# A set order for the first attention batch: scores ahead of attn x v, first keys copied in two parts, transposes and h blocks moved around its end

## Chip, cores, metric

The kernel runs on one core of a Trainium2 chip. The metric is the device time of one execution in microseconds (us). The span in a profile (first to last instruction) is about 1.8 us shorter than the time of the same execution.

## The reference

```python
def _attn_ref(q, k, v):                      # q, k, v: (8, 12, 448, 64)
    scores = scale * np.matmul(q, k.transpose(0, 1, 3, 2))
    attn = np.maximum(scores, 0.0) ** 2 / S
    return np.matmul(attn, v)

def _moe_ref(x, w_in, w_out):                # x: (3584, 768), w_in: (768, 2048), w_out: (2048, 768)
    h = x @ w_in
    r = np.maximum(h, 0.0)
    return (r * r) @ w_out
```

The attention output, laid out as 3584 x 768, is the x of the second function. The types taken and given are float32. The kernel works in float16 with float32 sums.

## The kernel before

A batch is three units (four heads each), a unit seven score tiles, so a batch has 21 tiles, 0 to 20. For each unit TensorE transposes q and k, and VectorE copies them out of PSUM, the memory that TensorE's results go to. For each tile TensorE makes the scores, ScalarE evicts them (copies them out of PSUM, here with relu, to float16), VectorE squares them, and TensorE multiplies them with v, summed over the seven tiles of the unit. Two copies then write x. The first batch has no other work to hide behind. Later batches lie among the matmuls of h (x @ w_in) and the output. The units 0 to 5 are transposed by TensorE; from unit 6 on, a transposing DMA transfer does it.

The parts that matter here (cuts marked `# ...`):

```python
def slot(dtype):                       # score and transpose buffers, two banks each
    slot_no[0] += 1
    third = not big and slot_no[0] % 3 == 2 and slot_no[0] < 29
    return (third_p if third else s_p).tile(...)

def pe_transpose(n):
    # ... 14 transposes of q and 14 of k into PSUM
        if n == 0:
            copy(i)                    # all seven blocks in one VectorE copy
            warm(1)                    # a filler matmul
    # ...
    if n == 3:
        return lambda: (copy(0, True), copy(1))   # ScalarE for q, VectorE for k

def score(t, times=1):
    # ... four matmuls, done `times` times over, then:
    nc.scalar.activation(out=at, in_=ps[:, :, 0:S], func=AF.Relu, scale=SK)

def visit(tiles, turn=None, lag=2, most=3):
    # ... first batch:
    for t in tiles:
        score(t, 2)                    # twice, which keeps TensorE busy
    if turn is not None:
        pe_transpose(turn)
    flush()
    av_some(lag, most)                 # attn x v of tiles that are two visits old
    for t in tiles:
        square(ats[t])
    flush()

warm(10)
pe_transpose(0)
for i in range(11):
    visit([t for t in (2 * i, 2 * i + 1) if t < NB0], turn={1: 1, 4: 2}.get(i))
    # ... loads
later = pe_transpose(3)
# ... loads of v and w_out, then of unit 6 and 7
av_some(1, 9)
some(f0[0:2])                          # f0, f1: h blocks 0 and 1, six matmuls each
later()
av_some(0, 9)
# ...
some(f0[2:4])
some(f1[0:2])
visit([NB0, NB0 + 1])                  # scores 21 and 22, of unit 3
```

## Time and profile before

| | before |
|---|---|
| time, median of 3 | 372.46 us (372.42 to 372.77) |
| span of the profile, granted TensorE clock | 370.7 us, 0.996 |
| first eviction of a score tile | 8.26 us |
| end of the 21st eviction | 26.26 us |
| scores 23 and 24 (the first after h block 2) | 31.51 us |
| first scores of unit 6 | 68.75 us |

Most of the reading of this profile is in the prediction below. What it leaves out is the seam after the batch. It is the continuation of the chain of waits that ended last (columns: start in us, length in us, what; `x4` counts instructions):

```profile
26.97 0.48 PE mm L423 x2
27.46 0.31 PE avt L273 x4
27.77 0.86 PE mm L423 x4
28.64 0.50 PE slot L255 x8
29.14 2.38 PE mm L423 x12
31.51 0.50 PE slot L255 x8
```

`mm` are h steps, `avt` is attn x v, `slot ... L255` are scores. TensorE stands nowhere here, so this stretch can be shortened only by moving work of it to an earlier time at which TensorE was idle. The start of the last row, 31.51 us, is the mark by which the two kernels can be compared, as from there on their order is the same.

### The profile page before, as it was taken

How to read it: one execution, taken by the hardware profiler on the slowest of the kernel's cores; microseconds unless marked ns; L12 is line 12 of the kernel's file. 1: busy time of each engine (PE TensorE's matmuls, PEld its weight loads, DVE VectorE, ACT ScalarE, POOL GpSimd, SP SyncE). 2: the span in 40 equal slices, each digit the busy share in tenths (PEclk: the TensorE clock that was granted, in tenths of full speed). 3: DMA queues.
4: the chain of work that ended last, by engine and by line, in shares of the span. 5: the costliest groups of instructions: out<-in, count | busy, mean ns of one | idle time of the engine just before them, and what ended most of it. 6: DMA issues, size and time to landing. Idle time of an engine off the chain costs nothing.

```text
span 370.7 us, 8742 instructions
## 1 busy us (share of the span) xinstructions
PE 361.1 (97%) x3600; PEld 230.9 (62%) x3600; DVE 266.0 (72%) x470; ACT 247.7 (67%) x370; POOL 107.1 (29%) x128
## 2 busy tenths in 40 slices
PE   8999999999999999999999999999999999999994
PEld 3554444445555778875555588887555689986663
DVE  1886677996767878798575766989756686884442
ACT  2997895786667999876555588887665885532220
POOL 8545531747542355522054045050000000000001
PEclk9999999999999999999999999999999999999998
DMA  8999999999999999969799999592233300002333
GB/s 116 195 204 205 205 204 170 126 146 161 190 170 137 185 106 104 108 90 73 137 136 108 176 162 94 82 104 48 54 82 88 87 1 2 2 0 79 91 91 83
DMA packets 121158, 42.63 MB, mean 115 GB/s; under 512 B 100832, under 2 KB 117760, under 8 KB 121120
## 3 DMA queue, kind: packets, MB, share of 16 engines
q0 software_dynamic: 82912, 23.01, 63.7%
q1 hardware_dynamic: 38048, 18.98, 25.8%
q8 instruction: 28, 0.46, 0.5%
q10 hardware_dynamic: 160, 0.10, 0.1%
q14 instruction: 10, 0.08, 0.1%
HBM read 45.61 MB, written 11.01 MB: 153 GB/s over the span
## 4 chain that ended last, share of the span: by engine, by line
PE 90%; ACT 4%; DVE 3%; issue 1%; POOL 0%; POOLq 0%; ACTq 0%
PE mm L739 34%; PE mm L552 27%; PE slot L255 10%; PE mm L423 9%; PE slot L320 7%; ACT at L259 4%; DVE at L372 1%; PE slot L204 1%; PE slot L226 1%; DVE xt L286 1%; PE mm L226 0%; DVE kT L217 0%; ACT u L641 0%; DVE osb L646 0%; PE avt L273 0%
## 5 line engine op out<-in xcount | busy, mean ns | idle before, releaser
L259 ACT ACTIVATE at<-slot 128x896 f16<-128x896 f32 x168 | 145.9, 919 | 27.9 <-PE slot L255 27.8
L372 DVE TENSOR_TENSOR at<-at 128x896 f16<-128x896 f16 x168 | 99.3, 618 | 12.1 <-ACT at L259 12.0
L109 POOL DMA_DIRECT2D qs<-in_q_dram x36 | 35.3, 983 | 116.5 <-DMA qT<-qs 108.7
L739 PEld LDWEIGHTS <-s 128*128 128x128 f16 x440 | 41.5, 98 | 32.7 <-issue 3.6
L255 PE MATMUL slot<-qT,kT 64*64 64x448 f16 x756 | 57.4, 360 | 1.6 <-ACT at L259 0.9
L552 PEld LDWEIGHTS <-w 128*128 128x128 f16 x576 | 54.3, 98 | 5.1 <-issue 4.3
L552 PE MATMUL mm<-xt,w 128*128 128x224 f16 x432 | 48.9, 259 | 0.0
L739 PEld LDWEIGHTS <-g 128*128 128x128 f16 x336 | 31.7, 98 | 24.1 <-issue 4.7
L552 PEld LDWEIGHTS <-ws 128*128 128x128 f16 x432 | 40.3, 98 | 4.7 <-issue 4.7
L646 DVE SCALAR_TENSOR_TENSOR osb<-mm,u 128x384 f32<-128x384 f32 (+1 forms) x30 | 16.2, 543 | 36.2 <-ACT u L641 23.7
L739 PE MATMUL mm<-b,g 128*128 128x384 f16 x224 | 40.7, 326 | 0.0
L739 PE MATMUL mm<-b,s 128*128 128x384 f16 x216 | 39.6, 326 | 0.2 <-DVE s L608 0.2
L423 PE MATMUL mm<-xt,w 128*128 128x448 f16 x192 | 39.8, 354 | 0.0
L739 PE MATMUL mm<-t,s 128*128 128x384 f16 x224 | 39.3, 326 | 0.0
L255 PEld LDWEIGHTS <-kT 64*64 64x64 f16 x756 | 19.6, 104 | 28.9 <-issue 23.6
L109 POOL DMA_DIRECT2D ks<-in_k_dram x36 | 35.1, 977 | 8.4 <-DMA b<-in_moe_w_out_dram 5.8
L575 POOL DMA_DIRECT2D out_dram<-osb x2 | 1.1, 564 | 119.7 <-DVE osb L646 119.7
L641 ACT ACTIVATE u<-mm 128x384 f32<-128x384 f32 x28 | 13.8, 492 | 31.3 <-PE mm L739 26.8
L552 PE MATMUL mm<-x,ws 128*128 128x224 f16 x288 | 34.1, 259 | 0.0
L495 DVE CUSTOM_DVE_ANT_0 g<-mm,m 128x448 f16<-128x448 f32 x36 | 22.4, 622 | 14.9 <-PE mm L552 7.2
L320 PE MATMUL slot<-at,vt 64*64 64x448 f16 x588 | 31.9, 350 | 0.2 <-DVE at L372 0.2
L501 DVE TENSOR_TENSOR g<-g 128x896 f16<-128x896 f16 x48 | 28.8, 618 | 0.4 <-ACT g L504 0.4
(68 smaller groups left out, 378.1 us busy)
## 6 DMA issues: line engine op xcount, KB each, us to landing
out_dram<-osb SPq DMA_DIRECT2D x52, 192.0 KB, 3.0
vt<-in_v_dram POOLq DMA_DIRECT2D x24, 224.0 KB, 6.0
qs<-in_q_dram POOLq DMA_DIRECT2D x36, 112.0 KB, 4.4
ks<-in_k_dram POOLq DMA_DIRECT2D x36, 112.0 KB, 5.2
w<-in_moe_w_in_dram POOLq DMA_DIRECT2D x8, 384.0 KB, 11.7
b<-in_moe_w_out_dram POOLq DMA_DIRECT2D x4, 768.0 KB, 17.1
q<-in_q_dram POOLq DMA_DIRECT2D x6, 224.0 KB, 7.6
k<-in_k_dram POOLq DMA_DIRECT2D x6, 224.0 KB, 8.1
```

Of the source, the lines that this page charges most:

```text
L109: nc.gpsimd.dma_start(out=t[:, :, hh, :], in_=heads(src, n)[:, hh].rearrange("p (j d) -> p j d", d=D))
L255: nc.tensor.matmul(ps[c, hh, 0:S], lhsT=kT[r, j, c], rhs=qT[r, :, c], start=True, stop=True)
L259: nc.scalar.activation(out=at, in_=ps[:, :, 0:S], func=AF.Relu, scale=SK)
L320: nc.tensor.matmul(ps[64 * hh:64 * hh + 64, hp, 0:S], lhsT=vt[r, hh, j * D:(j + 1) * D], rhs=at[r, hh, :], start=(j == 0), stop=(j == J - 1))
L372: lambda: nc.vector.tensor_mul(at, at, at), 0))
L423: nc.tensor.matmul(cell[0][:, 0:S], lhsT=w1[f // 4][:, m, (f % 4) * P:(f % 4 + 1) * P], rhs=xts[b][:, m, :], start=(m == 0), stop=(m == NM ...
L495: nc.vector._custom_dve(TENSOR_ADD_SAT, out=gs(s, hi, right), in0=acc(s, y), in1=keep[s, nm], s0=3.4e38, s1=0.0)
L501: lambda: nc.vector.tensor_mul(g, g, g), b))
L552: nc.tensor.matmul(XY[s][y][:, r * Q:(r + 1) * Q], lhsT=left(k, i0 + 2 * s + r, m), rhs=right(k, m), start=(fresh and r == 0 and m == 0), ...
L641: nc.scalar.activation(out=t, in_=X[0][:, 0:HALF], func=AF.Copy, scale=CO)
L646: nc.vector.scalar_tensor_tensor(out=osb[row][:, c], in0=acc[0][:, 0:cc.stop - cc.start], scalar=CO, in1=keep[nm][:, cc], op0=ALU.mult, op ...
L739: nc.tensor.matmul(acc[0][:, 0:HALF], lhsT=left()[:, f], rhs=right[:, f], start=(fresh and f == 0), stop=(f == KH - 1), skip_group_check=n ...
```

## The change

The loop over visits of the first batch is replaced by a list of calls. Its intent: let ScalarE begin sooner, never let it wait for a score, and give TensorE work while the last squares and copies run. The diff, cut to its core:

```diff
-    def slot(dtype):
-        slot_no[0] += 1
-        third = not big and slot_no[0] % 3 == 2 and slot_no[0] < 29
+    def slot(dtype, third=False):
...
+    def turn_first(ps):
+        ts = new_qkt()
+        for i, src in enumerate(q16s.pop(0)):
+            tps = slot(FP16)[:, i, 0:J * P].rearrange("p (j c) -> p j c", j=J)
+            # 14 transposes
+            if i:
+                nc.scalar.activation(out=ts[i][:, 0], in_=tps[:, 0], func=AF.Copy)
+            nc.vector.tensor_copy(ts[i][:, i:J], tps[:, i:J])
+            warm(ps, 1)
+        qkt[0] = ts
...
-            return lambda: (copy(0, True), copy(1))
+            return lambda: copy(0, True), lambda: copy(1)
...
-    for i in range(11):
-        visit([t for t in (2 * i, 2 * i + 1) if t < NB0], turn={1: 1, 4: 2}.get(i))
+    s(0, 1)          # s(t, times=2): a score; THIRD = (0, 3, 5, 8, 10, 13, 16, 19)
+    s(1)
+    s(2)
+    s(3)
+    square0(0, 1)
+    pe_transpose(1)
+    s(4, 1)
+    s(5)
+    square0(2)
+    av0(0, 1)
+    s(6)
+    square0(3)
+    s(7)
+    av0(2)
...                  # on in this way; s(9, 1) behind pe_transpose(2)
+    s(19)
+    later = pe_transpose(3)
+    square0(17)
+    s(20)
+    av0(14, 15, 16, 17)
+    square0(18, 19, 20)
+    later[0]()
...
-    av_some(1, 9)
-    some(f0[0:2])
-    later()
-    av_some(0, 9)
+    some(f0[0:4])
+    av0(18, 19, 20)
+    x0(2, 0, act=True)
+    x0(2, 1)
+    later[1]()
+    some(f1[0:4])
...
-    some(f0[2:4])
-    some(f1[0:2])
+    some(f0[4:6])
     visit([NB0, NB0 + 1])
```

More of the change, by code (lines that the diff above doesn't have):

```diff
@@ L192, with warm @@
     wsum: dict = {}
-    slot_no = [0]
-    def slot(dtype):
-        slot_no[0] += 1
-        third = not big and slot_no[0] % 3 == 2 and slot_no[0] < 29
+    def slot(dtype, third=False):
         return (third_p if third else s_p).tile(
             [P, 2, 2048 // mybir.dt.size(dtype)], dtype, name="slot", tag="slot")
-    def warm(n):
-        ps = slot(FP32)
+    def warm(ps, n):
         for _ in range(n):
@@ L205, in warm @@
                              start=True, stop=True)
+    def turn_first(ps):
+        ts = new_qkt()
+        for i, src in enumerate(q16s.pop(0)):
+            tps = slot(FP16)[:, i, 0:J * P].rearrange("p (j c) -> p j c", j=J)
+            for j in range(J):
+                for hh in range(2):
+                    nc.tensor.transpose(
+                        tps[64 * hh:64 * hh + 64, j],
+                        src[:, hh, j * D:(j + 1) * D], ident)
+            if i:
[3 more added lines that the diff above has]
+        qkt[0] = ts
     def pe_transpose(n):
@@ L221, in pe_transpose @@
         else:
-            pss = [ps, slot(FP16) if n == 0 else ps]
+            pss = [ps, ps]
         for i, src in enumerate(srcs):
@@ L228, in pe_transpose @@
                         src[:, hh, j * D:(j + 1) * D], ident)
-            if n == 0:
-                copy(i)
-                warm(1)
         qkt[n] = ts
         if n == 3:
-            return lambda: (copy(0, True), copy(1))
-        if n > 0:
-            copy(0, n > 3)
-            copy(1)
+            return lambda: copy(0, True), lambda: copy(1)
+        copy(0, n > 3)
+        copy(1)
     xts: dict = {}
@@ L243, with score @@
     now = [0]
-    av_order: deque = deque(range(NU * J))
     avt = [None]
-    def score(t, times=1):
+    def score(t, times=1, third=False):
         n, j = divmod(t, J)
         qT, kT = qkt[n]
-        ps = slot(FP32)
+        ps = slot(FP32, third)
         for hh in list(range(2)) * times:
@@ L261, in score @@
         seen[t] = now[0]
-    def av_round(t):
-        n, j = divmod(t, J)
-        b, u = divmod(n, NU)
-        vt, at = vts[n], ats.pop(t)
-        if j == 0:
-            avt[0] = [p.tile([P, 512], FP32, name="avt", tag="av") for p in av_ps]
-        ap = avt[0]
-        for hp in range(2):
-            r = slice(64 * hp, 64 * hp + 64)
-            for hh in range(2):
-                nc.tensor.matmul(
-                    ap[hp][64 * hh:64 * hh + 64, 0:S],
-                    lhsT=vt[r, hh, j * D:(j + 1) * D], rhs=at[r, hh, :],
-                    start=(j == 0), stop=(j == J - 1))
-        if j == J - 1:
-            if u == 0:
-                xts[b] = x_p.tile([P, NM, S], FP16, name="xt", tag="xt")
-            for hp in range(2):
-                dst = xts[b][:, 2 * u + hp, :]
-                if b < 2 and u == NU - 1 and hp == 0:
-                    nc.scalar.activation(
-                        out=dst, in_=ap[hp][:, 0:S], func=AF.Copy, scale=CX)
-                else:
-                    nc.vector.tensor_scalar(
-                        out=dst, in0=ap[hp][:, 0:S],
-                        scalar1=CX, scalar2=None, op0=ALU.mult)
@@ L290, in av_some, with av0 @@
-    def av_some(lag=2, most=3):
-        done = 0
-        while av_order and done < most:
-            t = av_order[0]
-            if t not in seen or seen[t] > now[0] - lag:
-                break
-            av_order.popleft()
-            av_round(t)
-            done += 1
-            if t % J == J - 1:
-                break
+    def av0(*tiles):
+        for t in tiles:
+            n, j = divmod(t, J)
+            vt, at = vts[n], ats.pop(t)
+            if j == 0:
+                avt[0] = [p.tile([P, 512], FP32, name="avt", tag="av") for p in av_ps]
+            for hp in range(2):
+                r = slice(64 * hp, 64 * hp + 64)
+                for hh in range(2):
+                    nc.tensor.matmul(
+                        avt[0][hp][64 * hh:64 * hh + 64, 0:S],
+                        lhsT=vt[r, hh, j * D:(j + 1) * D], rhs=at[r, hh, :],
+                        start=(j == 0), stop=(j == J - 1))
@@ new lines, in x0, with square0 @@
+    def x0(n, hp, act=False):
+        if 0 not in xts:
+            xts[0] = x_p.tile([P, NM, S], FP16, name="xt", tag="xt")
+        dst, src = xts[0][:, 2 * n + hp, :], avt[0][hp][:, 0:S]
+        if act:
+            nc.scalar.activation(out=dst, in_=src, func=AF.Copy, scale=CX)
+        else:
+            nc.vector.tensor_scalar(
+                out=dst, in0=src, scalar1=CX, scalar2=None, op0=ALU.mult)
+    def square0(*tiles):
+        for t in tiles:
+            nc.vector.tensor_mul(ats[t], ats[t], ats[t])
@@ L372, in square, with visit @@
                     lambda: nc.vector.tensor_mul(at, at, at), 0))
-    def visit(tiles, turn=None, lag=2, most=3):
+    def visit(tiles):
         now[0] += 1
@@ L378, in visit @@
                 prefetch(t // J + 2)
-        if big:
-            for t in tiles[:1]:
-                score(t)
-            av_unit()
-            for t in tiles[1:]:
-                score(t)
-            at_pe[0] += 0.19 + 0.19 * len(tiles)
-            for i, t in enumerate(tiles):
-                square(ats[t], 0.6 + 0.85 * i)
-            return
-        for t in tiles:
-            score(t, 2)
-        if turn is not None:
-            pe_transpose(turn)
-        flush()
-        av_some(lag, most)
-        for t in tiles:
-            square(ats[t])
-        flush()
+        for t in tiles[:1]:
+            score(t)
+        av_unit()
+        for t in tiles[1:]:
+            score(t)
+        at_pe[0] += 0.19 + 0.19 * len(tiles)
+        for i, t in enumerate(tiles):
+            square(ats[t], 0.6 + 0.85 * i)
     gts: dict = {}
@@ L789, with s @@
     NB0 = NU * J
-    warm(10)
-    pe_transpose(0)
-    for i in range(11):
-        visit([t for t in (2 * i, 2 * i + 1) if t < NB0], turn={1: 1, 4: 2}.get(i))
-        if i == 0:
-            load16(3)
-            load_w1(0)
-            load_w1(1)
-            load_v(3)
-        if i == 2:
-            load16(4)
-            load_w1(2)
-            load_v(4)
-        if i == 5:
-            load16(5)
-            load_w1(3)
-            load_v(5)
-    later = pe_transpose(3)
+    ps = slot(FP32, True)
+    warm(ps, 10)
+    turn_first(ps)
+    def s(t, times=2):
+        score(t, times, third=t in THIRD)
+    THIRD = (0, 3, 5, 8, 10, 13, 16, 19)
+    s(0, 1)
[4 more added lines that the diff above has]
+    pe_transpose(1)
+    load16(3)
+    load_w1(0)
+    load_w1(1)
+    load_v(3)
+    s(4, 1)
[6 more added lines that the diff above has]
+    av0(2)
+    square0(4)
+    s(8)
+    av0(3)
+    square0(5, 6)
+    pe_transpose(2)
+    load16(4)
+    load_w1(2)
+    load_v(4)
+    s(9, 1)
+    square0(7)
+    s(10)
+    av0(4, 5)
+    square0(8)
+    s(11)
+    av0(6)
+    x0(0, 0)
+    x0(0, 1)
+    square0(9)
+    load16(5)
+    load_w1(3)
+    load_v(5)
+    s(12)
+    s(13)
+    square0(10, 11)
+    s(14)
+    av0(7, 8, 9)
+    square0(12)
+    s(15)
+    av0(10)
+    square0(13)
+    s(16)
+    av0(11)
+    s(17)
+    av0(12, 13)
+    square0(14)
+    x0(1, 0)
+    x0(1, 1)
+    s(18)
+    square0(15, 16)
+    s(19)
+    later = pe_transpose(3)
+    square0(17)
[3 more added lines that the diff above has]
+    later[0]()
     load_v(6)
@@ L902 @@
         events.append((2 * T_H - (3 - i) * T_G, lambda i=i: outs[0][1](i)))
-    steps = [(0.1892, None, False)] * 6 + f1[2:4] + f0[4:6] + f1[4:6]
+    steps = [(0.1892, None, False)] * 10 + f1[4:6]
     for f in range(2, NF):
```

## The prediction

> **What bounds the kernel now.** I read the page first, then the chain of waits around the first batch, then each engine's timeline there, then the DMA queue up to the first use of data that comes through it late.
>
> The change touches only the first attention batch (21 score tiles) and its seam with the first h blocks, that is, the first 30 us of 370.7. Three engines' busy time in that stretch (engines: busy us, instructions in brackets):
>
> ```profile
> core 0: us, PE busy (x) PEld busy (x) DVE busy (x) ACT busy (x) POOL busy (x), PEclk, DMA share, GB/s
> 8.20:26.30 18.10, 16.13 (x320) 9.92 (x308) 15.63 (x29) 17.39 (x21) 9.17 (x14) 1.00 1.23 197
> ```
>
> ScalarE (ACT) is nearest to its limit, 17.39 of 18.10 us, all of it the 21 relu evictions of score tiles; VectorE (DVE) has 15.63 us for 29 instructions. So no order of work inside this stretch can win more than about 0.7 us: the rest must come from its start and its end. ScalarE's timeline (start, us, what, idle before) shows where its 0.7 us goes:
>
> ```profile
> 8.26 8.27 ACT L259 ACTIVATE at<-slot 128x896 f16<-128x896 f32 x10 [6.02 <-PE slot L255]
> 16.87 3.35 ACT L259 ACTIVATE at<-slot 128x896 f16<-128x896 f32 x4 [0.34 <-PE slot L255]
> 20.48 5.78 ACT L259 ACTIVATE at<-slot 128x896 f16<-128x896 f32 x7 [0.27 <-PE slot L255]
> 26.51 0.92 ACT L215 ACTIVATE qT<-slot 128x896 f16<-128x896 f16 x1 [0.25 <-PE slot L226]
> ```
>
> Ten evictions in 8.27 us with a last one of 0.92 give a pitch of (8.27 - 0.92)/9 = 0.82 us. Twenty pitches are 16.3 us; from 8.26 the 21st would start at 24.6 and it starts at 25.34 (20.48 + 6 x 0.81), so 0.7 us are gaps, behind the transposes of unit 2 and the x copies. The chain that ended last (start, us, what) says what follows:
>
> ```profile
> 7.64 0.60 PE slot L255 x8
> 8.24 0.02 issue
> 8.26 6.66 ACT at L259 x8
> ...
> 15.97 0.62 DVE qT L217
> 16.60 0.53 DVE kT L217
> 17.13 1.07 DVE at L372 x2
> 18.20 1.06 DVE xt L286 x2
> ...
> 24.49 0.97 ACT at L259
> 25.46 0.04 issue
> 25.50 0.97 PE slot L226 x28
> 26.47 0.50 PE avt L273 x8
> ```
>
> Before 25.5 the path runs through ScalarE and VectorE. From 25.50 on TensorE (PE) sets it: the transposes of unit 3 (0.97 us) stand after all 21 scores. From there it runs almost without a wait to the end of the kernel, so what is gained before about 30 us should be gained at the end, unless something arrives by a clock of its own. One thing does: DMA is fully busy from 4 to 62 us, and unit 6's keys come through it.
>
> ```profile
> 61.48 1.23 SPq L120 DMA_TRANSPOSE kT<-ks  x1
> DMA to landing us min/median/max: 5.8/5.8/5.8
> 68.75 0.50 PE slot L255 x8
> ```
>
> The first row is the issue of the transposing transfer of these keys, the second its time to landing (so 67.3), the third the matmuls that read them.
>
> **What the Trainium skill says.** "ScalarE: Activation LUTs", section "What ACT_TABLE_LOAD costs", puts an ACTIVATE at a fixed part plus 0.833 ns per element. The trace agrees: 0.919 us for 896 columns and 0.544 for 448, a slope of 0.837 ns and 0.17 us fixed, so an estimate of 0.28 us for the new copy of 128 columns. "PSUM — Partial Sum Buffer", section "PSUM bank collisions raise a hardware error", says two engines must not read one bank at once, so ScalarE's and VectorE's parts of the first key copy should run one after the other. No copy of before shows this. "TensorE: Matmul & The Clock Gate", section "The mechanism" of Part 3, says matmuls start and end in program order. The trace agrees: at 18.78 and 23.45 us the attn x v matmuls stood waiting for an x copy, and the scores behind them stood too (0.7 us of TensorE waits on x copies in three waits). That is what putting scores ahead of attn x v addresses.
>
> **The change, part by part.**
>
> Start. Before: keys transposed by 6.94, one VectorE copy of all seven key blocks 6.96 to 7.60, scores 7.64 to 8.24 (each computed twice, eight matmuls), first eviction 8.26. After: ScalarE copies block 0 alone, 6.96 to 7.24. TensorE is free from 7.21, after the filler matmul. Score 0 is computed once, four matmuls, 0.38 us: 7.27 to 7.65. First eviction 7.67, so 0.6 us earlier. VectorE copies the other six blocks, 7.26 to about 7.8, score 1 is ready at 8.4, and the second eviction is due at 7.67 + 0.82 = 8.49: no gap.
>
> Middle. The same instructions in a fixed order with three rotating score buffers, plus three scores computed once instead of twice (3 x 4 matmuls at about 0.05 us, 0.6 us off TensorE). I walked the order by hand with 0.82 per eviction, 0.54 per VectorE instruction, 0.97 per set of 28 transposes, 0.57 per double score. Each score found its buffer free and was ready before ScalarE asked, also behind the transposes of units 1 and 2 (at about 9.4 and 13.5 us; the data of unit 2 land at 13.3). So up to 0.7 us of gaps go. The last eviction then ends at 7.67 + 16.3 + 0.92 = 24.9 instead of 26.26. VectorE is close behind: 29 x 0.54 = 15.6 us from 8.6 on, plus about 1.3 us in which it waits for transposes and evictions, so the last square is done at about 25.5 (before: 26.9).
>
> End. The 28 transposes of unit 3 come before score 20, as soon as a buffer frees at about 22.5, while ScalarE still has three evictions to do. Four steps of h block 0 run before the last attn x v, four of block 1 after it. Then: last attn x v 25.9, x copies 26.6, VectorE's key copy 27.1, scores 21 and 22 to 27.6, last two steps of block 1 to 28.0. Before, h block 1 ended at 29.14 + 6 x 0.2 = 30.3. That is 2.3 us in a walk without any slip. A walk by hand misses semaphore delays and short queues, so I take 1.5 to 2.3, middle 1.8, of which 0.6 is the start, about 0.6 gaps, about 0.6 the end. No arithmetic of any size is removed.
>
> Downstream. From 30 us the order is as before, shifted. The first scores of unit 6 start at 68.7; their keys land at 67.3 by the DMA's clock. Their issue waited for data in a queue that has been full since 4 us, so the shift won't move it. The slack is 68.7 - 67.3 = 1.4 us. A shift of 1.8 would run into it by about 0.4, and a short semaphore and weight-load delay of about 0.1 comes on top. So I expect about 1.3 us to survive: 372.46 - 1.3 = 371.15.
>
> **The rivals.**
> First, the DMA does not cap it: the keys land earlier too, or only a part is needed, and all 1.8 us arrive, 370.7. Against: the landing of each transfer follows the bytes ahead of it at about 204 GB/s; for: a few instructions that free load buffers come earlier, and landing times could vary by half a microsecond.
> Second, VectorE takes ScalarE's place as the bound in the first batch. Its 15.63 us already lies on the chain at 16 to 21 us. If the late squares hold up the attn x v and those the x copies, the gaps come back and only the start's 0.6 us plus a little of the end remains: 371.7.
> Third, the wait moves: ScalarE's share of the key copy might make score 0 wait for the whole key tile, which would leave score 0 at 7.85 and make the start worse by 0.2 less 0.2 for the single computing. For region-wise waits speaks that h steps reading x blocks 2 and 3 ran at 27.70, ahead of the copies into blocks 4 and 5 (27.81 and 28.00), which stand before them in the program. That rival gives about 371.8.
> A slower kernel would need TensorE's clock to drop after fewer double scores; with 16.13 of 18.10 us busy before and 0.6 us less after, in three places, I see no pause long enough.
>
> **Range and chances.** Point 371.15, between the cap (1.3) and what survives if the first batch yields less. The low end, 370.6, is the full shift without a cap; the high end, 371.8, is the start alone. Two per cent is 7.4 us, more than the whole of what this stretch could give: within 2% is as good as certain, 0.98, and 0.01 for each side.
>
> **What would show each step right or wrong.** First eviction at about 7.7 us, a ScalarE copy of 0.28 us at about 7.0 and VectorE's part following it: the start. ScalarE's evictions in one run to about 25 us: the middle; gaps named after score matmuls would speak for the second rival. The end of h block 1 at 28.0 to 28.8 us instead of 30.3: the end. A TensorE wait of some tenths before the scores at about 67.3 us, released by the key transfer or by nothing visible: the cap; none there and a span shorter by over 1.5 us: the first rival. The prediction is wrong if the shift at 30 us is below 0.8 us, or if a shift over 1.5 us there reaches the end undiminished.

## The result, and the profile after

| | before | after |
|---|---|---|
| time, median of 4 runs each | 372.6 us | 370.66 us (370.6 to 371.21) |
| span, clock | 370.7 us, 0.996 | 368.9 us, 0.998 |
| first eviction | 8.26 us | 7.72 us |
| end of the 21st eviction | 26.26 us | 24.90 us |
| scores 23 and 24 | 31.51 us | 29.73 us |
| first scores of unit 6 | 68.75 us | 66.97 us |
| last part of the output matmuls | 364.31 us | 362.53 us |

The ratio is 0.9951, with a 95% interval of 0.9934 to 0.9969. Ratios here are the mean time of one kernel's fast runs over that of the other's of the same rounds, so not quite the ratio of the medians quoted. The kernel is about 0.5% faster, by the profile 1.8 us. The forecast was 1.3.

Busy time in the first batch after (same columns as in the prediction), from 0.12 us before the first eviction to 0.5 us behind the end of the last (the 22nd ScalarE instruction is the copy of unit 3's queries):

```profile
7.60:25.40 17.80, 16.00 (x316) 10.05 (x312) 16.04 (x30) 17.68 (x22) 9.55 (x15) 1.00 1.23 195
```

ScalarE now has 17.68 of 17.80 us: by busy time it is full. Its timeline shows the 21 evictions as one row, where before had three rows with 0.34 and 0.27 us between them (a row ends only where the engine stands idle, so a short delay can hide in it; see "The middle" below):

```profile
6.96 0.28 ACT L214 ACTIVATE kT<-slot 128x128 f16<-128x128 f16 x1 [4.72 <-PE slot L210]
7.72 17.18 ACT L266 ACTIVATE at<-slot 128x896 f16<-128x896 f32 x21 [0.49 <-PE slot L262]
24.80 0.91 ACT L227 ACTIVATE qT<-slot 128x896 f16<-128x896 f16 x1
```

The first row is the new small copy. VectorE's part of the key copy follows it and does not overlap it:

```profile
7.27 0.56 DVE L215 COPY kT<-slot 128x768 f16<-128x768 f16 x1 [0.70 <-ACT kT L214]
```

The chain of waits around the end of the batch after:

```profile
22.46 0.97 PE slot L238 x28
23.43 0.50 PE slot L262 x8
23.94 0.76 PE avt L280 x16
24.69 0.86 PE mm L409 x4
25.55 0.69 PE avt L280 x12
26.25 1.26 PE mm L409 x6
27.50 0.03 issue
27.54 0.57 PE slot L262 x8
28.11 1.62 PE mm L409 x8
29.73 0.50 PE slot L262 x8
```

The transposes of unit 3 (first row) start at 22.46 instead of 25.50, and from there TensorE runs without a pause to scores 23 and 24 at 29.73.

The 1.78 us divide as follows. The first eviction is 0.54 us earlier (8.26 to 7.72). From its start to the end of the 21st eviction it takes 17.18 us instead of 18.00, so 0.82. The mark at 31.51 moved to 29.73, which leaves 1.78 - 0.54 - 0.82 = 0.42 us for the end. The same 1.78 us stand at the scores of unit 6 and at the output's last part: nothing is lost on the way. The cap that the prediction put at 67.3 us did not act. The issue of the transposing transfer of unit 6's keys, its time to landing, and the scores that read them:

```profile
61.88 1.23 SPq L120 DMA_TRANSPOSE kT<-ks  x1
DMA to landing us min/median/max: 4.4/4.4/4.4
66.97 0.50 PE slot L262 x8
```

The issue did not come earlier; it came 0.4 us later than before (61.48). But the transfer landed after 4.4 us instead of 5.8, at 66.3, and 0.7 us of slack remained: the keys lay ready 0.7 us before the scores that read them.

### The profile page after: what moved, and what is told of

Read it like the earlier page. It is cut to its first block, busy times and chain, and to the rows that moved or that the text cites. A ratio compares the mean times of both kernels' runs of the same rounds, so it can differ in the third digit from the quotient of the medians.

```text
span 368.9 us, 8720 instructions
## 1 busy us (share of the span) xinstructions
PE 359.6 (97%) x3588; PEld 230.3 (62%) x3588; DVE 265.4 (72%) x470; ACT 247.5 (67%) x371; POOL 107.1 (29%) x128
## 4 chain that ended last, share of the span: by engine, by line
PE 90%; ACT 3%; DVE 3%; issue 2%; DMA 1%; POOL 0%; POOLq 0%; ACTq 0%
PE mm L725 34%; PE mm L538 27%; PE slot L262 10%; PE mm L409 9%; PE slot L317 7%; ACT at L266 3%; DMA k<-in_k_dram 1%; DVE at L297 1%; PE avt L280 1%; PE slot L238 1%; PE mm L238 0%; DVE at L369 0%; DVE xt L292 0%; ACT u L627 0%; DVE osb L632 0%
## 5 line engine op out<-in xcount | busy, mean ns | idle before, releaser
L369 DVE TENSOR_TENSOR at<-at 128x896 f16<-128x896 f16 x147 | 87.1, 617 | 9.7 <-ACT at L266 9.6
L538 PEld LDWEIGHTS <-w 128*128 128x128 f16 x576 | 54.3, 98 | 5.1 <-issue 4.3
L409 PEld LDWEIGHTS <-w 128*128 128x128 f16 x192 | 17.1, 98 | 19.2 <-issue 5.1
```

The lines of the kernel that those rows point to most:

```text
L369: lambda: nc.vector.tensor_mul(at, at, at), 0))
L409: nc.tensor.matmul(cell[0][:, 0:S], lhsT=w1[f // 4][:, m, (f % 4) * P:(f % 4 + 1) * P], rhs=xts[b][:, m, :], start=(m == 0), stop=(m == NM ...
L538: nc.tensor.matmul(XY[s][y][:, r * Q:(r + 1) * Q], lhsT=left(k, i0 + 2 * s + r, m), rhs=right(k, m), start=(fresh and r == 0 and m == 0), ...
```

## The experiments

All twelve kernels gave correct results. The table gives the median of each and the marks of its profile. "Batch" is the time from the first eviction to scores 23 and 24: 23.25 us before, 22.01 after. It takes out the start, which moves by some tenths from profile to profile with the landing of the first keys. "Slower by the medians" below is measured against the changed kernel's median in again, 370.69. best2 ran on another chip than the other eleven.

| kernel | median us | before, same rounds | ratio | batch us | scores of unit 6 | keys: issue + landing = landed |
|---|---|---|---|---|---|---|
| again | 370.69 | 372.52 | 0.9957 | 22.00 | 66.8 | 62.37 + 4.4 = 66.8 |
| start_only | 372.11 | 372.52 | 0.9987 | 23.26 | 68.05 | 62.27 + 5.7 = 68.0 |
| mid_old | 371.44 | 372.52 | 0.9973 | 22.82 | 67.7 | 61.50 + 4.4 = 65.9 |
| t3_late | 371.07 | 372.52 | 0.9964 | 22.43 | 67.7 | 62.79 + 4.4 = 67.2 |
| h_old | 371.25 | 372.52 | 0.9966 | 22.51 | 67.5 | 61.55 + 4.4 = 66.0 |
| k_whole | 370.95 | 372.52 | 0.9966 | 22.00 | 67.2 | 61.49 + 4.4 = 65.9 |
| dbl0 | 370.87 | 372.52 | 0.9960 | 22.00 | 67.1 | 61.46 + 4.4 = 65.9 |
| dbl49 | 371.11 | 372.52 | 0.9967 | 22.13 | 67.26 | 61.44 + 5.8 = 67.2 |
| dma_after | 371.07 | 372.55 | 0.9964 | 22.01 | 67.1 | 62.61 + 4.4 = 67.0 |
| dma_before | 372.53 | 372.55 | 1.0006 | 23.25 | 68.6 | 63.24 + 4.4 = 67.6 |
| best | 370.79 | 372.55 | 0.9954 | 21.99 | 67.0 | 61.56 + 4.4 = 66.0 |
| best2 | 370.51 | 372.42 | 0.9956 | 21.82 | 66.43 | 57.81 + 8.1 = 65.9 |

The intervals of the ratios are about 0.0013 to 0.0022 to each side, that is 0.5 to 0.8 us. So differences of some tenths between these kernels rest on their medians together with the marks of the profiles, not on the intervals. One cause of the width is that single executions fall on a second level some 0.4 to 0.7 us higher, whatever the kernel. In the first job before had 372.19 to 372.55 seven times and 372.93 and 373.07 once each. Single executions lie higher still (372.71 in k_whole, 372.36 in best2).

One reading settles which kernels lost time to unit 6's keys: the scores of unit 6 start 37.24 to 37.26 us after scores 23 and 24 in thirteen of the fourteen profiles, and 37.42 us after them in dbl49.

### again: the changed kernel once more

No edit.

> The changed kernel once more, unchanged. Theory (the 1.8 us won by 30 us reach the end, because the keys of unit 6 happened to land within reach): 1.7 to 1.95 us faster than before, the scores of unit 6 starting at 66.9 to 67.1 us. Rival (the landing of these keys varies from run to run and caps the gain in some executions): the keys land anywhere between 66 and 67.4 us, and single executions are 0.3 to 0.6 us longer than the best.

Measured: 370.69 us, 1.83 below before by the medians. The keys landed at 66.8 us, just when the scores of unit 6 came (66.8), so the slack was used up, at no cost: they start 37.25 us after scores 23 and 24, as elsewhere. Two of five executions were longer (371.02 and 371.17; the others 370.65 to 370.69). That agrees in form with the rival, but before has the same second level, and its slack is larger. So the longer executions are no sign of the cap.

### start_only: only the start of the change

```diff
+                if i:
+                    nc.scalar.activation(out=d3[:, 0], in_=p3[:, 0], func=AF.Copy)
+                nc.vector.tensor_copy(d3[:, i:J], p3[:, i:J])
                 warm(1)
...
-            score(t, 2)
+            score(t, 2 if t else 1)
```

(in the kernel before; `d3` and `p3` are views of the key tile and of its PSUM)

> The kernel before with only the start of the change: ScalarE copies the first key block, score 0 computed once. Theory (the start's 0.54 us are worth themselves, and the gaps and the end are separate gains): first eviction at 7.7 us, 0.4 to 0.6 us faster than before. Rival (VectorE bounds the middle anyway, so an earlier start only opens wider gaps in ScalarE): first eviction at 7.7 us, but under 0.2 us faster.

Measured: 0.41 us faster than before by the medians, first eviction at 7.53. In its profile the first eviction and scores 23 and 24 are 0.73 and 0.72 us earlier than before, as its first keys came 0.19 us earlier. ScalarE's timeline has the very gaps of before:

```profile
7.53 8.27 ACT L263 ACTIVATE at<-slot 128x896 f16<-128x896 f32 x10 [0.49 <-PE slot L259]
16.14 3.35 ACT L263 ACTIVATE at<-slot 128x896 f16<-128x896 f32 x4 [0.34 <-PE slot L259]
19.75 5.77 ACT L263 ACTIVATE at<-slot 128x896 f16<-128x896 f32 x7 [0.27 <-PE slot L259]
```

So an earlier start shifts the batch as a whole (23.26 us against 23.25), and the gaps are a separate matter. The theory holds.

### mid_old: the old order in the middle

The list from score 0 to score 17 in the order of the old visits, for instance:

```diff
-    s(8)
-    av0(3)
-    square0(5, 6)
-    pe_transpose(2)
-    s(9, 1)
-    square0(7)
-    s(10)
-    av0(4, 5)
+    s(8)
+    s(9, 1)
+    pe_transpose(2)
+    av0(4, 5)
+    square0(8, 9)
+    s(10)
```

> The changed kernel with the middle of the batch in the old order of tiles, attn x v and squares (start and end as changed). Theory (the set order closes ScalarE's gaps): gaps of 0.4 to 0.8 us come back in the row of 21 evictions, last eviction at 25.3 to 25.7 instead of 24.9, 0.4 to 0.8 us slower than the changed kernel. Rival (the gaps came from scores computed twice behind transposes, which this version keeps single): no gap over 0.1 us, within 0.15 us of the changed kernel.

Measured: 0.75 us slower than the changed kernel by the medians, 0.81 in the batch. The gaps are back, at the same places and of the same size as before, although three scores are computed once:

```profile
7.63 8.21 ACT L266 ACTIVATE at<-slot 128x896 f16<-128x896 f32 x10 [0.49 <-PE slot L262]
16.17 3.35 ACT L266 ACTIVATE at<-slot 128x896 f16<-128x896 f32 x4 [0.34 <-PE slot L262]
19.79 5.84 ACT L266 ACTIVATE at<-slot 128x896 f16<-128x896 f32 x7 [0.27 <-PE slot L262]
```

What makes the second gap is seen on TensorE. An attn x v there waits for the x copy to free its accumulator, and the scores behind it in the program start only after it:

```profile
18.09 0.38 PE L280 MATMUL avt<-at,vt 64*64 64x448 f16 x2 [0.38 <-DVE xt L292]
18.62 0.76 PE L280 MATMUL avt<-at,vt 64*64 64x448 f16 x10 [0.15 <-DVE xt L292]
19.03 1.10 PE L262 MATMUL slot<-qT,kT 64*64 64x448 f16 x16
```

ScalarE's gap at 19.5 us lies just behind these rows. The first gap, at 15.8 us, has another cause: score 10 stands behind the transposes of unit 2 (from 14.27) and eight attn x v matmuls (from 15.17), and starts at 15.57. In both places it is the order that makes ScalarE wait. The theory holds; the rival falls for these two gaps (dbl49 shows what the single scores are worth).

### t3_late: the transposes of unit 3 after score 20

```diff
-    later = pe_transpose(3)
     square0(17)
     s(20)
+    later = pe_transpose(3)
     av0(14, 15, 16, 17)
```

> The changed kernel with the transposes of unit 3 after score 20, as before. Theory (TensorE sets the path from 22.5 us on, and these transposes then start when the next buffer frees, at 23.3): h block 1 ends about 0.25 us later, 0.2 to 0.4 us slower than the changed kernel. Rival (the squares of the last tiles set the end, at 25.6 us, whatever TensorE does before): within 0.1 us of the changed kernel.

Measured: 0.38 us slower by the medians, as expected, and 0.42 in the batch. TensorE's timeline shows how:

```profile
22.71 0.57 PE L262 MATMUL slot<-qT,kT 64*64 64x448 f16 x8 [0.24 <-ACT at L266]
23.52 0.58 PE L238 MATMUL slot<-ident,q 128*64 128x128 f16 x14 [0.24 <-ACT at L266]
```

Score 20 takes the buffer that frees first, takes 0.57 us on TensorE, and the transposes then wait 0.24 us for the next. In the changed kernel the transposes take the first buffer, and score 20's wait for the second one falls into the transposes' own 0.97 us.

### h_old: the h blocks as before

```diff
-    some(f0[0:4])
+    some(f0[0:2])
     av0(18, 19, 20)
...
-    some(f1[0:4])
...
-    some(f0[4:6])
+    some(f0[2:4])
+    some(f1[0:2])
     visit([NB0, NB0 + 1])
```

(the remaining steps behind the scores, as in the kernel before)

> The changed kernel with the steps of h blocks 0 and 1 around the last attn x v and the scores of unit 3 as before (two steps ahead of the last attn x v, four after, the rest behind scores 21 and 22). Theory (h steps fill TensorE while the last square, the x copies and the last key copy run; without them it stands): TensorE idle 0.4 to 0.8 us between 25 and 27.6 us, 0.4 to 0.7 us slower than the changed kernel. Rival (the same steps are done later in the same queue, where they fill other waits): under 0.15 us slower.

Measured: 0.56 us slower by the medians, 0.50 in the batch. The chain of waits leaves TensorE here, as TensorE has too few h steps to do while the last x copy and the key copy run:

```profile
25.17 0.87 PE avt L280 x12
26.05 0.02 issue
26.07 0.62 DVE xt L292
26.69 0.54 DVE kT L229
27.23 0.04 issue
27.28 0.57 PE slot L262 x8
```

Score 21 starts earlier than in the changed kernel (27.28 against 27.54), and still the mark behind the h steps is later, as four of the ten steps that the changed kernel has done by then are still to do. TensorE's idle time before score 21 is 0.42 us, within what was expected.

### k_whole, dbl0: the two parts of the start

```diff
-            if i:
-                nc.scalar.activation(out=ts[i][:, 0], in_=tps[:, 0], func=AF.Copy)
-            nc.vector.tensor_copy(ts[i][:, i:J], tps[:, i:J])
+            nc.vector.tensor_copy(ts[i][:, 0:J], tps[:, 0:J])
```

> The changed kernel with the first keys copied whole by VectorE. Theory (the start shifts everything up to the end of the batch one to one): first score at 7.64 instead of 7.29, first eviction at 8.05 instead of 7.72, 0.3 to 0.35 us slower than the changed kernel. Rival (VectorE, not ScalarE, sets the end of the batch; its first squares come later but its total has room): under 0.15 us slower.

```diff
-    s(0, 1)
+    s(0)
```

> The changed kernel with score 0 computed twice. Theory (score 0 is on the path): first eviction at 7.9 instead of 7.72, 0.15 to 0.25 us slower than the changed kernel. Rival (the 0.5 us that the second score waits for the other key blocks absorbs it): no difference over 0.05 us.

Measured: 0.26 and 0.18 us slower by the medians. The starts of the first keys' copy and of the first eviction are 6.96 and 7.72 in the changed kernel (0.76 us apart), 6.83 and 7.94 in k_whole (1.11), 6.88 and 7.83 in dbl0 (0.95). That is 0.35 and 0.19 us. The rest of the batch is unchanged in both (22.00). Both theories hold; only k_whole's 0.26 by the medians is just under its expected 0.3 to 0.35.

### dbl49: the other two scores computed twice

```diff
-    s(4, 1)
+    s(4)
...
-    s(9, 1)
+    s(9)
```

> The changed kernel with the two scores behind the transposes of units 1 and 2 computed twice, as before. Theory (ScalarE asks for these scores 0.2 to 0.3 us after they are ready even when doubled by 0.19 us, so they are not on the path): within 0.1 us of the changed kernel. Rival (this is what closed the gaps): gaps of 0.1 to 0.2 us at the fifth and the tenth eviction, 0.2 to 0.4 us slower.

Measured: 0.42 us slower by the medians, outside what the theory expected and just above the rival's range. The rival is right about the place: by the start times in the trace, the fifth eviction starts 0.89 us after the fourth and the tenth 0.91 after the ninth, where the changed kernel has 0.80 in both. So each is late by about 0.1 us, too little to show as an idle time, and the 21 evictions take 17.30 us instead of 17.18; the batch is 0.12 us longer. But the large gaps stay closed, so the single scores are not what closed those. Another 0.17 us came 40 us later. The chain of waits shows it, the only one of these profiles in which it goes through the transfer of unit 6's keys:

```profile
61.44 5.77 DMA kT<-ks
67.21 0.04 issue
67.26 0.57 PE slot L262 x8
```

and TensorE's timeline names the wait:

```profile
67.26 0.57 PE L262 MATMUL slot<-qT,kT 64*64 64x448 f16 x8 [0.17 <-DMA kT<-ks]
```

dbl0, run in the same job, had score 21 at the same time (27.64), the keys after 4.4 us, the scores of unit 6 at 67.08, and was 0.24 us faster. The batch and the wait make 0.29 of the 0.42 us; the rest is within the spread of the medians. So this is the cap of the prediction, at the time it gave (67.3 us), in a kernel in which the transfer took as long as before. It was not made on purpose, which is why it shows the mechanism but not what decides between 4.4 and 5.8.

### dma_after, dma_before: one more load ahead of unit 6

```diff
+    ex = v_ex.tile([P, 2, J * D], FP16, name="ex", tag="ex")
+    nc.gpsimd.dma_start(out=ex, in_=heads(v, 6))
     load_qk(6)
```

> The changed kernel with one more load of 224 KB (written size, a copy of unit 6's v that nothing reads) put into the DMA queue just ahead of the loads for unit 6. At 204 GB/s it takes 1.1 us. Theory (a cap by the DMA's clock exists, the changed kernel is only short of it by the 0.7 us between the landing of unit 6's keys at 66.3 and their use at 67.0): keys land at 67.2 to 67.6, TensorE waits 0.3 to 0.6 us before the scores of unit 6, 0.3 to 0.7 us slower than the changed kernel. Rival (these transfers have slack that the landing times do not show): no wait there, same time as the changed kernel.

> The kernel before with the same additional load. Theory (slack of 1.4 us between landing at 67.3 and use at 68.7): no wait or under 0.2 us before the scores of unit 6, within 0.2 us of the kernel before. Rival (the additional load costs by itself): 0.3 us slower or more here too.

Measured: the load cost before nothing (372.53 against 372.55; keys at 67.6, used at 68.6). In the changed kernel the keys landed at 67.0, 0.7 us later than without it, and were used at 67.1, 37.24 us after scores 23 and 24, so without a wait. The median was 0.38 us above that of the changed kernel in the job of again, but the four executions were 370.82, 370.85, 371.3 and 371.3, so on both levels, and the profile's span was 369.1 against 368.9, of which 0.1 is a later first eviction. The load took up the slack and hardly more. As a test of the cap this is inconclusive after; before agrees with the theory.

### best: the first key block in a bank of its own

```diff
+            both = slot(FP16)
+            tps, own = [both[:, z, 0:J * P].rearrange("p (j c) -> p j c", j=J) for z in (i, 0)]
             for j in range(J):
                 for hh in range(2):
                     nc.tensor.transpose(
-                        tps[64 * hh:64 * hh + 64, j],
+                        (own if j == 0 else tps)[64 * hh:64 * hh + 64, j],
                         src[:, hh, j * D:(j + 1) * D], ident)
+                if i and j == 0:
+                    nc.scalar.activation(out=ts[i][:, 0], in_=own[:, 0], func=AF.Copy)
...
-            warm(ps, 1)
+            if not i:
+                warm(ps, 1)
...
-    s(20)
+    s(20, 1)
```

> An attempt to go further: the first key block is transposed into a PSUM bank of its own, so that ScalarE copies it while the other six are still being transposed; no filler matmul behind the keys; score 20 computed once. Theory (the start shifts the batch one to one, and score 20 is on TensorE's path): first score at about 6.95 and first eviction at 7.35 instead of 7.72, score 20 saves 0.19 us, together 0.4 to 0.6 us faster than the changed kernel if the keys of unit 6 land by 66.4, about 0.1 to 0.3 if they land at 67.3. Rival (the data of units 1 and 2, landing at about 9.1 and 13.3 us, now hold up their transposes, or VectorE is the bound): first eviction earlier, but under 0.15 us faster.

Measured: 370.79 us, not faster. Neither theory nor rival foresaw why. TensorE's timeline:

```profile
6.22 0.25 PE L211 MATMUL slot<-ident,k 128*64 128x128 f16 x2
6.83 0.53 PE L211 MATMUL slot<-ident,k 128*64 128x128 f16 x12 [0.37 <-ACT kT L215]
7.29 0.38 PE L264 MATMUL slot<-qT,kT 64*64 64x448 f16 x4
```

The other twelve transposes waited 0.37 us for ScalarE's copy, although they write another bank: the program orders accesses by the whole PSUM tile, and both banks were one tile. The next version, with two tiles, bears this out: there the twelve start at 6.40, right after the first two at 6.32. First score and first eviction came as late as in the changed kernel (7.29 and 7.72), and the second score later, as VectorE's part of the keys was late.

### best2: mended, with unit 6's loads moved ahead

```diff
+            own = tps
+            if i:
+                own = av_ps[0].tile([P, 1024], FP16, name="avt", tag="av")[
+                    :, 0:J * P].rearrange("p (j c) -> p j c", j=J)
...                  # the rest of the start and s(20, 1) as in the version above
-    load_w2(b21, 1, 0)
     load_qk(6)
+    load_w2(b21, 1, 0)
     load_qk(7)
```

> The previous attempt mended: the first key block is transposed into a PSUM tile of its own (the idle bank of an attn x v accumulator), so its copy by ScalarE cannot hold up the transposes of the other six; score 20 once; and the loads for unit 6 stand ahead of the last weight load in the DMA queue. Theory (start passes one to one to the end; score 20 is on TensorE's path; nothing of unit 6 waits for DMA any more): first eviction 0.35 us nearer to the first key transpose than in the changed kernel (1.05 instead of 1.39 us after it starts), score 21 about 0.15 us nearer to the first eviction, keys of unit 6 landing 3 us or more before their use, 0.4 to 0.6 us faster than the changed kernel, median near 370.2. Rival (data of units 1 and 2, or VectorE, bound the batch as soon as the start is earlier): first eviction earlier as said, but gaps of 0.1 us or more open in ScalarE's row, and under 0.2 us faster.

Measured: the first eviction came at 7.37, 1.05 us after the first key transpose, as expected, with no gap in ScalarE's row:

```profile
6.61 0.28 ACT L218 ACTIVATE kT<-avt 128x128 f16<-128x128 f16 x1 [4.37 <-PE avt L214]
7.37 17.11 ACT L271 ACTIVATE at<-slot 128x896 f16<-128x896 f32 x21 [0.49 <-PE slot L267]
```

The batch is 0.19 us shorter (score 20 once), and the scores of unit 6 stand at 66.43, 0.54 us ahead of the changed kernel. At the output's last part 0.37 of them are left (362.16 against 362.53); where the other 0.17 went I did not follow up. The median is 370.51 (370.25 three times to within 0.06, 370.72, 370.86 and one of 372.36), against 370.69 and 370.66 for the changed kernel in other jobs, the 370.69 on another chip. The ratio, 0.9956, does not part it from again (0.9957). By the profile and by the lowest executions it is 0.4 us faster. By the medians it is not shown. One expectation fell: the keys were issued 4.1 us sooner than in the changed kernel, yet landed only 0.4 us sooner, at 65.9, as the transfer took 8.1 us. The loads that now stood behind it ran at the same time. The Trainium skill's "DMA: Bandwidth & Descriptors", section "Issuing engines are not separate DMA queues", says that transfers of all issuing engines run on the same 16 DMA engines and interleave, and this agrees: from 57.8 to 66 us, 0.87 MB of other loads moved beside 0.46 MB of transposes.

## Why the prediction was right, and where not

The gain lies within the stated range, but by the prediction's own sign ("a shift over 1.5 us there reaches the end undiminished") it was wrong in one step, the cap downstream, and its first rival, 370.7, is what came. The range held because it had this rival at its low end.

**The bound.** Right. ScalarE was the limit in the batch, and after the change it is busy for 17.68 of 17.80 us. But "no more than about 0.7 us" inside the batch was too small; see the middle.

**The start** (said: 0.6, first eviction 7.67). It was 0.54, at 7.72. ScalarE's copy took 0.28 us, as estimated. VectorE's part of the keys followed ScalarE's as said (7.27 after 6.96 to 7.24). That it did so because of the bank is not shown: the program's own order by the whole tile, seen in best, would do the same. start_only, k_whole and dbl0 show that the copy in two parts is worth 0.35 us and the single score 0.19, and that both pass one to one through the batch. The third rival, that score 0 waits for the whole key tile, fell: score 0 began at 7.29, as VectorE's part began.

**The middle** (said: gaps of up to 0.7 go, about 0.6 in the sum). It was 0.82, more than the 0.7 that the prediction took for the limit. The prediction's term was mis-sized: it counted idle time, and took its pitch of 0.82 from a row that hides a late start (the fifth eviction, 0.89 us after the fourth). By the start times in the trace, evictions that wait for nothing start 0.80 us apart although each takes about 0.92, so neighbours overlap by about 0.12, and a gap costs roughly its idle time and that overlap: the gaps shown as 0.34 and 0.27 cost 0.50 and 0.41. Without any delay 21 evictions take 20 x 0.80 + 0.92 = 16.92 us; before took 18.00, so about 1.1 was to be had. After the change 0.26 is left, 0.05 at the eleventh eviction and 0.21 at the last, whose score now stands behind the transposes of unit 3. mid_old shows that the order of attn x v, squares and scores closes the two large gaps; dbl49 shows that the single scores 4 and 9 add 0.12 of the 0.82. The second rival, VectorE as the new bound, fell.

**The end** (said: about 0.6). It was 0.42. h block 1 ended at about 28.5 us, within the 28.0 to 28.8 that were said, but not at the 28.0 of the walk by hand. The early transposes and the h steps each matter: undone alone they cost 0.42 and 0.50 us of the batch. Together with mid_old's 0.81 this is 1.73 us, more than the 1.24 us by which the batch shrank (23.25 to 22.01). The parts need each other, so their shares do not add up.

**The sum.** The shift at 30 us was 1.78, and 1.8 was said. That this is so close is in part luck: the middle gave 0.2 more than said and the end 0.2 less. (The middle of "1.5 to 2.3" would have been 1.9, and 372.46 - 1.3 is 371.16.) TensorE's granted clock did not drop: 0.996 before, 0.998 after.

**Downstream** (said: unit 6's keys land at 67.3 by the DMA's clock, the slack is 1.4 us, and about 1.3 of 1.8 us survive). This is the step that failed. All of the 1.78 us reached the end. The half of the step about the issue was right in that it did not come earlier with the batch, though it is no fixed time either: 61.88 and 62.37 in two profiles of the changed kernel. The half about the landing was wrong: I took 5.8 us from issue to landing as fixed, from the one transfer of before. In the fourteen profiles it was 4.4 us in ten, 5.7 to 5.8 in three (before, start_only, dbl49), and 8.1 in best2, whose queue had another order. The mechanism of the cap exists, as dbl49 shows with its wait at 67.26. It did not act in the changed kernel, as its transfer landed at 66.3.

What decides between 4.4 and 5.8 stays open. It is not the order of the batch, as the kernel before with one more load had 4.4. One thing goes with it: in the three profiles with 5.7 to 5.8, the DMA engines stood nearly still (0 to 10 GB/s) from about 3.4 to 4.6 us after the issue, and the keys landed only after that; in the ten with 4.4 they moved over 130 GB/s all the time from 2.4 us after the issue to the landing. So the 1.4 us more are for the most part a pause, and not a slower transfer. The same stretch in before and in the changed kernel (columns as in the prediction, GB/s last):

```profile
65.00:66.00 1.00, 1.00 (x7) 0.54 (x6) 1.00 (x2) 0.54 (x1) 0.00 (x0) 1.00 0.06 6
```

```profile
65.00:66.00 1.00, 1.00 (x7) 0.50 (x6) 1.00 (x2) 0.41 (x2) 0.08 (x1) 1.00 1.28 255
```

Which is cause and which is effect these runs do not tell, nor whether a kernel always has the same of the two: each has one profile, only the changed kernel two (both 4.4). What the second level of times, 0.4 to 0.7 us higher, comes from is open too.

## What to carry to other kernels

Where an engine starts its work in program order, put the work that feeds the fullest engine ahead of work that may wait for a third engine. A gap in the fullest engine can come from this order alone, though no engine is too slow, and then a new order closes it at no cost. Measure such gaps by the times between starts: a list of idle times can hide short delays and the overlap that a gap destroys. Move what the next stage needs (transposes, first steps of the next product) to where the feeding engine would otherwise wait, and expect such moves to depend on each other. Before counting a gain at the front as a gain at the end, look for data that come by another clock, but do not take the landing time of a single transfer as that clock: its spread belongs in the range.

## What the Trainium skill lacked or had wrong

- "DMA: Bandwidth & Descriptors", section "DMA Transpose (X-bar)": it gives no time from issue to landing for a transposing transfer among other loads, nor does the rest of the page. Here the same transfer took 4.4 us in ten profiles, 5.7 to 5.8 in three, and 8.1 with more loads running beside it.
- "PSUM — Partial Sum Buffer", section "PSUM bank collisions raise a hardware error": it asks for order by bank and quadrant. The program here was ordered more coarsely, by the whole tile: in best, twelve transposes into one bank waited 0.37 us for a copy out of the other bank of the same tile, and in best2, with two tiles, they did not. No page that was read says that two banks need two tiles to be independent in such a program.
